# The output's transposes moved from TensorE to VectorE, in 32x32 blocks, with stores in 256-byte pieces

## The chip, the cores and the metric

The kernel runs on one core of a Trainium2 chip. The metric is device time in microseconds (us) of that core, as the median over several executions.

A core has five engines that matter here: TensorE (PE, with its weight loads shown as PEld), VectorE (DVE), ScalarE (ACT), GpSimd (POOL) and SyncE (SP), which issues most of the DMA transfers (1026 of 1214 in the trace of the kernel before).

## The reference

```python
X = np.fft.rfft(x, axis=1)                      # x: 8 batches x 3008 tokens x 256, fp32
y = np.fft.irfft(X * (filt_r + 1j * filt_i), n=3008, axis=1)
h = y.reshape(24064, 256) @ w_in                # w_in: 256 x 2048
g = np.where(h > 0, h, np.exp(np.minimum(h, 0)) - 1)
out = g @ w_out                                 # w_out: 2048 x 256, out: 24064 x 256
```

The kernel does the Fourier filter as matmuls with tables, and the two large products by a seven-product (Strassen-like) scheme.

## The kernel before

Its main loop has 192 steps, called quarters here: 8 batches, 6 groups of 512 tokens (448 in the first group), 4 quarters of the hidden layer. In each quarter PE interleaves seven groups of w_in matmuls (up: "U", into pha, phb, phc, phd, which are banks of PSUM, the memory that receives matmul results) with seven groups of w_out matmuls of the quarter before (down: "D", into po). DVE and ACT do the sums and the activation (ELU, the g of the reference) between them.

```python
for k in "UDUDUDUUD":            # first part of a quarter
    ...
for fn, a in plan.get((i, 0), ()):   # place 0: work planned here, as o_unit
    fn(*a)
for k in "UDUDD":                # second part: s3 (phc again), D, s4 (phd again), D, D
    ...
# in up_steps, in this order: s5: add("t4", mm(5, "c", True), g["t2"])     reads phc
#                             s7: add("b22", mm(7, "d", True), g["t4"])    reads phd
#                             s3: add("b12", mm(3, "c", False), g["t2"])   mm accumulates into phc
```

After the fourth quarter of a group, DVE forms c, the group's result with output columns on the partitions and tokens along the free dimension. One quarter later, at place 0, the output unit puts it the other way round and stores it. There are 48 units; the first is in quarter 5, and then there is one in every fourth quarter.

```python
def o_unit(b, m):
    c = cs_.pop((b, m))                               # two tiles [128, 512]
    for a in range(2):
        ps = psM.tile([P, 2, D], FP32, tag="mx", name="pso")
        o = op.tile([P, 2, D], FP32, tag="o%d" % a, name="o%d" % a)
        ...
                nc.tensor.transpose(ps[0:w, u, ts(dh, P)], c[dh][:, ds((2 * a + u) * P, w)], eye)
        nc.scalar.activation(out=o[:, 0:full, :], in_=ps[:, 0:full, :], func=AXT.Copy)
        ...
                nc.sync.dma_start(raw(out, ...), r[:, u:u + w, :])    # rows of 1 KB
```

## Time and profile before

The median of three runs is 2761.48 us (2761.05 to 2762.83).

| engine | busy us | share of the span |
|---|---|---|
| PE | 2667.8 | 97% |
| DVE | 2017.9 | 73% |
| ACT | 1332.3 | 48% |
| all DMA queues | | about 31% of 16 engines' time |

From the page, the chain that ended last by line, and the DMA queue of SyncE and its kin (packets, MB, share of 16 engines):

```profile
PE po L385 37%; PE pha L312 11%; PE phc L312 11%; PE phd L312 11%; PE phb L312 5%; PE psa L167 3%; PE psn L266 2%; PE psr L211 2%; PE pva L211 2%; PE pso L424 2%; DMA z<-t 1%; DVE g L317 1%; ACT e L323 1%; ACT e L324 1%; DVE c L403 1%
...
q1 hardware_dynamic: 122656, 173.60, 24.6%
```

The chain is matmuls almost throughout. The transposes (pso) have 2% of it, so that is about the most that their removal can bring. DMA is far from full.

### The profile page before, as it was taken

How to read it: one execution, taken by the hardware profiler on the slowest of the kernel's cores; microseconds unless marked ns; L12 is line 12 of the kernel's file. 1: busy time of each engine (PE TensorE's matmuls, PEld its weight loads, DVE VectorE, ACT ScalarE, POOL GpSimd, SP SyncE). 2: the span in 40 equal slices, each digit the busy share in tenths (PEclk: the TensorE clock that was granted, in tenths of full speed). 3: DMA queues.
4: the chain of work that ended last, by engine and by line, in shares of the span. 5: the costliest groups of instructions: out<-in, count | busy, mean ns of one | idle time of the engine just before them, and what ended most of it. 6: DMA issues, size and time to landing. Idle time of an engine off the chain costs nothing.

```text
span 2761.7 us, 36475 instructions
## 1 busy us (share of the span) xinstructions
PE 2667.8 (97%) x13376; PEld 2281.5 (83%) x13376; DVE 2017.9 (73%) x3427; ACT 1332.3 (48%) x2281; POOL 275.3 (10%) x325
## 2 busy tenths in 40 slices
PE   3689999999999999999999999999999999999998
PEld 1278778987899878998789877898789987899887
DVE  4877877777776777767776787767877677777776
ACT  2244455544455444554454544454454544554544
POOL 4311210002000120001200021000210012000000
PEclk7599999999999999999999999999999999999999
DMA  9644421434114331242313332143321223110100
GB/s 243 180 115 120 106 56 29 118 87 99 43 47 117 77 90 37 72 114 71 78 50 87 87 89 66 37 106 94 98 61 39 72 69 94 37 39 19 25 22 16
DMA packets 141634, 214.51 MB, mean 78 GB/s; under 512 B 25268, under 2 KB 99142, under 8 KB 141456
## 3 DMA queue, kind: packets, MB, share of 16 engines
q1 hardware_dynamic: 122656, 173.60, 24.6%
q0 software_dynamic: 17792, 36.93, 5.5%
q8 instruction: 106, 1.74, 0.3%
q10 hardware_dynamic: 1008, 1.64, 0.2%
q14 instruction: 72, 0.59, 0.1%
HBM read 137.04 MB, written 78.12 MB: 78 GB/s over the span
## 4 chain that ended last, share of the span: by engine, by line
PE 86%; DVE 7%; ACT 3%; DMA 2%; issue 2%; ACTq 0%; DVEq 0%; POOL 0%; SPq 0%
PE po L385 37%; PE pha L312 11%; PE phc L312 11%; PE phd L312 11%; PE phb L312 5%; PE psa L167 3%; PE psn L266 2%; PE psr L211 2%; PE pva L211 2%; PE pso L424 2%; DMA z<-t 1%; DVE g L317 1%; ACT e L323 1%; ACT e L324 1%; DVE c L403 1%
## 5 line engine op out<-in xcount | busy, mean ns | idle before, releaser
L385 PE MATMUL po<-g,wo 128*128 128x256 f32 (+1 forms) x5376 | 1324.2, 375 | 0.0
L385 PEld LDWEIGHTS po<-g,wo 128*128 128x128 f32 x5376 | 1021.4, 190 | 116.2
L323 ACT ACTIVATE e<-g 128x512 f32<-128x512 f32 (+1 forms) x576 | 357.6, 621 | 600.5 <-DVE g L317 600.3
L324 ACT ACTIVATE e<-e 128x512 f32<-128x512 f32 (+1 forms) x768 | 477.6, 622 | 24.4
L312 PE MATMUL pha<-y,wi 128*128 128x256 f32 (+1 forms) x1536 | 396.6, 381 | 9.3 <-ACT g L332 9.1
L317 DVE TENSOR_TENSOR g<-phc,g 128x512 f32<-128x512 f32 (+1 forms) x384 | 259.8, 677 | 197.5 <-PE phc L312 197.5
L328 DVE SCALAR_TENSOR_TENSOR g<-e,g 128x512 f32<-128x512 f32 (+1 forms) x576 | 387.5, 673 | 11.6 <-ACT e L324 11.2
L323 ACT ACTIVATE e<-pha 128x512 f32<-128x512 f32 (+1 forms) x192 | 113.0, 588 | 532.2 <-PE pha L312 532.2
L312 PEld LDWEIGHTS pha<-y,wi 128*128 128x128 f32 x1536 | 285.4, 191 | 93.4 <-ACT t L238 34.3
L317 DVE TENSOR_TENSOR g<-phd,g 128x512 f32<-128x512 f32 (+1 forms) x384 | 261.2, 680 | 86.4 <-PE phd L312 65.7
L328 DVE SCALAR_TENSOR_TENSOR g<-e,pha 128x512 f32<-128x512 f32 (+1 forms) x192 | 129.5, 674 | 259.7 <-ACT e L324 259.7
L227 POOL TENSOR_TENSOR sr<-sr,sp 128x512 f32<-128x512 f32 x64 | 80.9, 1264 | 1303.7 <-DVE sp L225 1303.7
L312 PE MATMUL phc<-ys,wi 128*128 128x256 f32 (+1 forms) x768 | 195.5, 377 | 2.8 <-DVE si L224 2.8
L312 PE MATMUL phd<-y,wi 128*128 128x256 f32 (+1 forms) x768 | 195.2, 377 | 1.3
L312 PE MATMUL phb<-ys,wi 128*128 128x256 f32 (+1 forms) x768 | 194.1, 375 | 0.0
L312 PE MATMUL phc<-y,wi 128*128 128x256 f32 (+1 forms) x768 | 194.0, 375 | 0.0
L312 PE MATMUL phd<-ys,wi 128*128 128x256 f32 (+1 forms) x768 | 193.7, 375 | 0.0
L312 PEld LDWEIGHTS phc<-ys,wi 128*128 128x128 f32 x768 | 145.3, 191 | 24.0 <-issue 8.1
L312 PEld LDWEIGHTS phd<-y,wi 128*128 128x128 f32 x768 | 145.2, 191 | 22.5 <-PE phc L312 6.5
L332 ACT ACTIVATE g<-pha 128x512 f32<-128x512 f32 (+1 forms) x192 | 112.7, 587 | 105.7 <-PE pha L312 105.5
L312 PEld LDWEIGHTS phb<-ys,wi 128*128 128x128 f32 x768 | 146.0, 190 | 17.1 <-issue 0.5
L312 PEld LDWEIGHTS phd<-ys,wi 128*128 128x128 f32 x768 | 145.8, 190 | 16.5
(108 smaller groups left out, 2787.9 us busy)
## 6 DMA issues: line engine op xcount, KB each, us to landing
z<-t SPq DMA_DIRECT2D x192, 128.0 KB, 3.9
t<-z SPq DMA_DIRECT2D x128, 192.0 KB, 3.7
yd<-t SPq DMA_DIRECT2D x128, 192.0 KB, 2.8
t<-yd SPq DMA_DIRECT2D x192, 128.0 KB, 4.2
out_dram<-o SPq DMA_DIRECT2D x176, 128.0 KB, 2.4
xc<-in_x_dram SPq DMA_DIRECT2D x84, 256.0 KB, 4.6
f<-fd POOLq DMA_DIRECT2D x112, 192.0 KB, 3.6
tn<-tn_t SPq DMA_DIRECT2D x48, 256.0 KB, 4.1
```

The source lines that it names most:

```text
L167: nc.tensor.matmul(ps[:, u, :], w[:, r + u, :], xt[:, r + u, :], start=True, stop=True)
L211: nc.tensor.matmul(ps[:, u:u + w, :], table[k, v, :], rhs[k, u:u + w, :], start=True, stop=True)
L227: nc.gpsimd.tensor_tensor(out=sr, in0=sr, in1=p, op=ALU.subtract)
L266: nc.tensor.matmul(ps[:, ts(q, P)], t[:, i - 4 * m, ds(dh * P, P)], w[:, i - 4 * m, :], start=True, stop=True)
L312: nc.tensor.matmul(banks[key][:, a, 0:h], w_in[q][:, COMBO[n], a, :], y[n], start=start and a == 0, stop=True, skip_group_check=True)
L317: nc.vector.tensor_tensor(out=g[o], in0=i0, in1=i1, op=ALU.add)
L323: nc.scalar.activation(out=e, in_=src, func=AXT.Relu, scale=-1.0)
L324: nc.scalar.activation(out=e, in_=e, func=AXT.Exp, scale=-1.0)
L328: nc.vector.scalar_tensor_tensor(out=g[n], in0=es[n], scalar=1.0, in1=src, op0=ALU.subtract, op1=ALU.max)
L332: nc.scalar.activation(out=g["t1"], in_=mm(1, "a", True), func=AXT.Copy)
L385: nc.tensor.matmul(po[i][:, u, 0:h], w_out[q][:, COMBO[n], a, :], g[n][:, a, :], start=q == 0 and a == 0 and n in (1, 3, 6, 4), stop=True, ...
L424: nc.tensor.transpose(ps[0:w, u, ts(dh, P)], c[dh][:, ds((2 * a + u) * P, w)], eye)
```

## The change

The intent is to take the transposes off PE, the engine that bounds the kernel, and the copies off ACT. The new layout takes a DVE transpose of 128x512 fp32 to turn each 32x32 block by itself, inside its group of 32 partitions. After that, partition group a (32 partitions) holds, for 32 tokens at a time, 32 columns from each half of c. The columns of w_out are therefore laid out so that these 64 columns are neighbours in the output, columns 64a to 64a+63. A token's 1 KB row then lies in four partition groups and leaves in four pieces of 256 bytes, in separate DMA issues: 16 or 24 stores of 32 KB a unit (24 KB and 8 KB in the first group), where there were 4 or 5 of mostly 128 KB.

```diff
-    eye = glob.tile([P, P], FP32, name="eye")
...
-            c = [kp.tile([P, 512], FP32, tag="c%d" % i, name="c%d" % i) for i in range(2)]
+            c = kp.tile([P, 2, 512], FP32, tag="c", name="c")
...
     def o_unit(b, m):
         c = cs_.pop((b, m))
-        for a in range(2):
-            ps = psM.tile([P, 2, D], FP32, tag="mx", name="pso")
...
-                    nc.tensor.transpose(ps[0:w, u, ts(dh, P)], c[dh][:, ds((2 * a + u) * P, w)], eye)
-            nc.scalar.activation(out=o[:, 0:full, :], in_=ps[:, 0:full, :], func=AXT.Copy)
...
+        o = op.tile([P, 16, 2, 32], FP32, tag="o", name="o")
+        for j, n in ((0, 8), (8, 6 if m == 0 else 8)):
+            nc.vector.transpose(out=o[:, j:j + n], in_=c[:, :, ds(32 * j, 32 * n)].rearrange("p e (j s) -> p j e s", s=32))
+        o = o.rearrange("p (u f k) e s -> p u f k (e s)", u=4, f=2)
...
+                for k in range(2):
+                    for a in range(4):
+                        nc.sync.dma_start(raw(out, b * N + n1 + 32 * N1 * k,
+                                              [[N1 * D, 32], [-D if f else D, w], [1, 64]], 64 * a),
+                                          o[ts(a, 32), u:u + w, f, k])
...
-            f, e = (t.rearrange("p (i c) -> p i c", i=4) for t in (f, e.bitcast(FP32)))
+            f, e = (t.rearrange("p (i a e s) -> p i e a s", i=2, a=4, e=2) for t in (f, e.bitcast(FP32)))
+            dst = dst.rearrange("p (i e) (a s) -> p i e a s", i=2, a=4)
```

More of the change, by code (lines that the diff above doesn't have):

```diff
@@ L110 @@
     ]
-    id_d = nc.inline_tensor(np.eye(P, dtype=np.float32), name="id_t").ap()
     def pool(name, bufs, **kw):
@@ L142, with raw @@
     xs, tas, tns, t1s, t2s, ss, t3s, t4s, zs, yds, ys, g_of, po_of, cs_ = ({} for _ in range(14))
-    def raw(src, row, ap):
-        return bass.AP(tensor=src.tensor, offset=src.offset + row * D, ap=ap)
+    def raw(src, row, ap, col=0):
+        return bass.AP(tensor=src.tensor, offset=src.offset + row * D + col, ap=ap)
     def x_load(b, c, queue=nc.sync, place=None):
@@ L398, in tail @@
             p35, p7 = (k[1][:, u, 0:h] for u in range(2))
-            c = [kp.tile([P, 512], FP32, tag="c%d" % i, name="c%d" % i) for i in range(2)]
-            (c11, c12), (c21, c22) = ((t[:, 0:h], t[:, h:2 * h]) for t in c)
+            c = kp.tile([P, 2, 512], FP32, tag="c", name="c")
+            (c11, c12), (c21, c22) = ((c[:, i, 0:h], c[:, i, h:2 * h]) for i in range(2))
             def add(o, i0, i1):
@@ L416, in o_unit @@
         c = cs_.pop((b, m))
-        for a in range(2):
-            ps = psM.tile([P, 2, D], FP32, tag="mx", name="pso")
-            o = op.tile([P, 2, D], FP32, tag="o%d" % a, name="o%d" % a)
-            full = 1 if m == 0 and a == 1 else 2
-            for u in range(2):
-                w = P if u < full else 64
-                for dh in range(2):
-                    nc.tensor.transpose(ps[0:w, u, ts(dh, P)], c[dh][:, ds((2 * a + u) * P, w)], eye)
-            nc.scalar.activation(out=o[:, 0:full, :], in_=ps[:, 0:full, :], func=AXT.Copy)
-            if full == 1:
-                nc.scalar.activation(out=o[0:64, 1, :], in_=ps[0:64, 1, :], func=AXT.Copy)
-            i0, i1 = order(m)[2 * a:2 * a + 2]
-            for f in range(2):
-                r = o[f * 64:f * 64 + 64]
-                for u, w in ((0, 2),) if i1 == i0 + 1 else ((0, 1), (1, 1)):
-                    i = (i0, i1)[u]
-                    if f and i == 0:
-                        continue
-                    n1 = N1 - i if f else i
-                    nc.sync.dma_start(raw(out, b * N + n1, [[N1 * D, 64], [-D if f else D, w], [1, D]]), r[:, u:u + w, :])
+        o = op.tile([P, 16, 2, 32], FP32, tag="o", name="o")
+        for j, n in ((0, 8), (8, 6 if m == 0 else 8)):
+            nc.vector.transpose(out=o[:, j:j + n], in_=c[:, :, ds(32 * j, 32 * n)].rearrange("p e (j s) -> p j e s", s=32))
+        o = o.rearrange("p (u f k) e s -> p u f k (e s)", u=4, f=2)
+        for u, w, i in ((0, 3, 1), (3, 1, 0)) if m == 0 else ((0, 4, 4 * m),):
+            for f in range(1 if i == 0 else 2):
+                n1 = N1 - i if f else i
+                for k in range(2):
[3 more added lines that the diff above has]
+                                          o[ts(a, 32), u:u + w, f, k])
     wds = {}
@@ L468, in w_convert @@
         m, e = (kp.tile([P, 512], U32, tag=t, name=n) for t, n in (("k0", "wm"), ("k1", "we")))
-        f, l = (kp.tile([P, 512], FP32, tag=t, name=n) for t, n in (("c0", "wf"), ("c1", "wl")))
+        fl = kp.tile([P, 2, 512], FP32, tag="c", name="wfl")
+        f, l = fl[:, 0], fl[:, 1]
         nc.vector.tensor_scalar(out=m, in0=hi, scalar1=0x000FFFFF, scalar2=None, op0=ALU.bitwise_and)
@@ L485, in w_convert @@
         else:
-            f, e = (t.rearrange("p (i c) -> p i c", i=4) for t in (f, e.bitcast(FP32)))
-        nc.vector.tensor_tensor(out=dst, in0=f, in1=e, op=ALU.mult)
+            f, e = (t.rearrange("p (i a e s) -> p i e a s", i=2, a=4, e=2) for t in (f, e.bitcast(FP32)))
+            dst = dst.rearrange("p (i e) (a s) -> p i e a s", i=2, a=4)
+        if shape:
+            nc.vector.tensor_tensor(out=dst, in0=f, in1=e, op=ALU.mult)
+        else:
+            for i in range(2):
+                nc.vector.tensor_tensor(out=dst[:, i], in0=f[:, i], in1=e[:, i], op=ALU.mult)
         if j % 2 == 1:
@@ L578 @@
             w_fetch(k)
-        nc.scalar.dma_start(eye, id_d)
         n_unit(0, 0)
```

## The prediction

> **What bounds the kernel now.** I read the page first: the busy shares, then the chain of waits that ended last.
>
> ```profile
> PE 2667.8 (97%) x13376; PEld 2281.5 (83%) x13376; DVE 2017.9 (73%) x3427; ACT 1332.3 (48%) x2281; POOL 275.3 (10%) x325
> ...
> PE 86%; DVE 7%; ACT 3%; DMA 2%; issue 2%; ACTq 0%; DVEq 0%; POOL 0%; SPq 0%
> ```
>
> TensorE holds 86% of the chain, and its 40 slices read 9 from the fourth on. What counts is time between matmul starts, not the busy sum. From about 215 us on, starts are 216 ns apart for a 256-column matmul, and the gaps above the usual pace sum to about 25 us over the remaining 2540 us, outside the filter matmuls. Time taken out of PE's stream there shortens the run one for one, unless something else is late at that point.
>
> Next, the groups by shape, for the two instructions that go, and the issues of the output tile:
>
> ```profile
> L424 PE MATMUL pso<-eye,c 128*128 128x128 f32 x368 | 48.5, 273 | 2.0 <-DVE g L317 1.2 <-DVE c L403 0.7
> ...
> L425 ACT ACTIVATE o<-pso 128x512 f32<-128x512 f32 x88 | 47.3, 584 | 3.7 <-PE pso L424 3.7
> ...
> L436 SPq DMA_DIRECT2D out_dram<-o x200: 467/604/2078, 218.7 to 2757.9; - x100
> ```
>
> The mean of 273 ns is a transpose's length; its cost is in the timeline of PE around one output unit, then of DVE there:
>
> ```profile
> 1258.60 1.03 PE L385 MATMUL po<-g,wo 128*128 128x256 f32 x4
> 1259.46 1.04 PE L424 MATMUL pso<-eye,c 128*128 128x128 f32 x8
> 1260.34 1.03 PE L312 MATMUL phc<-y,wi 128*128 128x256 f32 x4
> ...
> 1259.06 0.69 DVE L317 TENSOR_TENSOR g<-phc,g 128x512 f32<-128x512 f32 x1
> 1259.85 0.69 DVE L317 TENSOR_TENSOR g<-phd,g 128x512 f32<-128x512 f32 x1
> 1261.40 0.69 DVE L317 TENSOR_TENSOR g<-phc,g 128x512 f32<-128x512 f32 x1 [0.86 <-PE phc L312]
> ```
>
> Eight transposes hold PE from 1259.46 to 1260.34, 0.87 us, 109 ns each. I measured this at all 48 units: 0.87 us at 46, 1.19 at the first, and the last lies in the tail. On DVE, an add reads bank phc and ends at 1259.75, and after the next add DVE is idle 0.86 us until PE has filled phc again. The new transposes go into that idle slot. But the PE group that follows, the second one into phc, accumulates into the bank the first add reads, so it cannot start before 1259.75. Today the transposes cover that.
>
> Last, the tail:
>
> ```profile
> 2754.46 0.42 DVE L403 TENSOR_TENSOR c<-k,k 128x256 f32<-128x256 f32 x1
> ...
> 2755.19 1.08 ACT L425 ACTIVATE o<-pso 128x512 f32<-128x512 f32 x2 [3.65 <-PE pso L424]
> 2755.81 2.71 SPq L436 DMA_DIRECT2D out_dram<-o  x4
> ```
>
> The last block of c is complete at 2754.88, the last of four stores is issued at 2757.9, and the span ends at 2761.7.
>
> [...] No transpose on DVE is in this trace; the 128x512 fp32 add[...] takes 677 ns, so I take 0.68 us for a 128x512 transpose, an estimate. [...] The trace has no 256 B stores; its 1 KB packets take 46 ns at the median.
>
> **The change part by part.**
> *Removed from PE:* 384 transposes. In the stream 47 units x 0.87 = 40.9 us; the 48th is in the tail.
> *Removed from ACT:* 104 copies, some 53 us, on no path except once in the tail. Two PSUM buffers per unit are also no longer taken from the shared pool of four. I went through the rotation: a later group gets its bank from an earlier one in every case, or one freed some 4 us before it is wanted. Neither gain nor loss.
> *Added to DVE:* 96 transposes of 0.68 us, 65 us in all, DVE from 73% to about 76%. Per unit, two of them start 0.6 us apart[...].
> *What PE gives back:* without the transposes the second phc group waits for the add into t4 that reads phc. Relative to the start of the transposes, that add ends in an ordinary batch at -0.67, +0.29, -0.16, -0.16, +0.10 and -0.41 us over the six units. A wait also costs some 0.15 us: 0.05 from the release to the start (seen in the tail) and 0.1 because the weight load is no longer hidden (PE groups of four after a wait last 1.13 us instead of 1.03). So two units of six lose: 0.44 + 0.25 = 0.69 us a batch, 4.8 us over seven batches. In the last batch, where TensorE has less other work, five units lose (0.51, 0.29, 0.28, 0.28, 0.26, each + 0.15): 2.4 us; the unit before them 0.6; and at the first unit (1.14 late) all 0.87 is lost. Sum 8.7 us. PE's net gain is 40.9 - 8.7 = 32.2 us.
> *What DVE's delay does:* the next add from phc starts after the transposes, at about +2.4 us instead of +1.94, and PE is up to 0.87 us earlier, so it is late by about 0.9 us against PE. The add after it, from phd, is late by about 0.4. What PE needs next from these are the combined operands: b22 about 3 us, t1 about 2.8 us before its matmul in the ordinary quarter. DVE waits for ACT or PE between 1 and 3 us in each quarter, so it catches up. I count nothing.
> *Stores:* 104 a batch of 32 KB instead of 25 of mostly 128 KB: 832 issues for 200. The issue's median is 0.6 us with 128 pieces, and the new ones also have 128 pieces. A burst of 16 keeps the SyncE queue for about 10 us of a quarter of 12 to 14. The loads and the spectrum stores behind it come later by up to 8 us, but they are issued two quarters (about 26 us) before use. Nothing in the steady part.
> *Tail:* two transposes after 2754.88 (1.3 us), then 15 issues of 0.6 us before the last: issued 10.4 us after c is complete, instead of 3.0. The stretch from there to the end stays 3.8 us. Tail: +7.4 us.
> *Weights:* eight products for w_out become two of half size, 0.7 instead of 0.6 us; about five are on the chain at the start: +0.5 us.
> Sum: 2761.5 - 32.2 + 7.4 + 0.5 = 2737. I leave 1 us for what I did not see: 2738.
>
> **Rivals.**
> First, *DVE becomes the limit*. For it: in the quarters with filter products DVE has 13 operations of 0.6 to 0.7 us, four products and, one in four, seven adds and a transposed unit, about 12 us on average of PE's 14. If the fp32 transpose took twice my estimate, a unit would add 2.8 us on DVE. Against it: PE's operands come nearly 3 us early. It would make 2745 to 2765.
> Second, *the stores stop the SyncE queue*. For it: at the start the spectrum stores take 1.1 us per issue instead of 0.58[...]; 16 x 1.1 is 17.6 us, longer than a quarter, and loads would then slip from unit to unit. Against it: the queue waits in more than half of the span (859 us of it for the ACT copies of the output), and DMA is 30% busy. Four times the packets would add some 3 to 6% of DMA time, if a 256 B packet costs between half and all of a 1 KB one. It would make 2745 to 2790.
> Third, *PE gets all 41 us back*, because DVE in its turn moves forward with PE: 2728 with the tail, 2720 if the tail costs nothing.
>
> **Range and chances.** A gain of over 2% needs less than 2706 us, and all of the transposes with no tail give 2720: 2%. Over 2% slower means 2817, which takes a queue that stops PE some 1.7 us per unit beyond all that it saves: 3%. Within 2%: 95%. The range, 2722 to 2760, has the third rival at its lower end and mild forms of the other two at its upper.
>
> **What would show it right or wrong.** The group pso is gone from PE. After the po group, the second phc group starts with no gap at four units of six and with a gap of 0.3 to 0.4 us at two, released by DVE's add. The DVE transposes last about 0.68 us, and DVE's idle time before the next phc add disappears. SyncE's stores show 16 issues of about 0.6 us, and the last is issued about 10 us after c is complete. I am wrong if a transpose lasts well over 1 us, if an issue of a store takes over 1 us in the steady part, if PE's gaps behind z, t or yd loads grow, or if gaps at combined operands (g on DVE) appear in the quarter after a unit.

## The result, and the profile after

The changed kernel takes 2734.93 us (2733.8 to 2735.32, 4 runs) against 2761.5 us, 26.6 us less. The ratio is 0.9902, 95% interval 0.9885 to 0.9919: a clear gain of 1%, within the 2% that counts as the same. A ratio is the mean time of one kernel's runs over that of the other's of the same rounds, so it is not quite the ratio of the medians.

In the page after, the busy shares, the chain by engine, and the DMA queue (the changed kernel's line numbers are about two lower in the main loop: L310 for L312, L315 for L317, L383 for L385):

```profile
PE 2626.5 (96%) x12992; PEld 2237.5 (82%) x12992; DVE 2066.9 (76%) x3531; ACT 1286.0 (47%) x2177; POOL 275.6 (10%) x325
...
q1 hardware_dynamic: 210592, 173.65, 25.8%
...
PE 77%; DVE 12%; ACT 5%; DMA 2%; issue 2%; POOL 0%; DVEq 0%; SPq 0%; ACTq 0%; POOLq 0%
```

PE has lost exactly the 384 transposes (13376 less 12992) and 41 us of busy time; DVE has gained 49 us. The chain goes through DVE more often, 12% of the span instead of 7%: there are now places where PE waits for DVE, and a chain that follows such a wait back stays on DVE for a while. SyncE's queue moved 88 thousand packets more for 1.2 points of DMA time.

The new instructions, first the DVE transposes in the groups by shape (count, busy us, mean ns, idle before):

```profile
L421 DVE STREAM_TRANSPOSE o<-c 128x512 f32<-128x512 f32 x88 | 57.4, 687 | 0.2
```

Then the stores, in the view of tile o (count, then ns of one issue: least, median, most):

```profile
L429 SPq DMA_DIRECT2D out_dram<-o x832: 315/430/2152, 216.7 to 2730.9; - x167
```

The timeline of PE, then of DVE, around the unit that the prediction shows (start, us):

```profile
1244.55 1.03 PE L310 MATMUL phd<-y,wi 128*128 128x256 f32 x4
1245.41 1.03 PE L383 MATMUL po<-g,wo 128*128 128x256 f32 x4
1246.61 1.13 PE L310 MATMUL phc<-y,wi 128*128 128x256 f32 x4 [0.17 <-DVE g L315]
...
1245.87 0.68 DVE L315 TENSOR_TENSOR g<-phc,g 128x512 f32<-128x512 f32 x1
1246.66 0.69 DVE L315 TENSOR_TENSOR g<-phd,g 128x512 f32<-128x512 f32 x1
1247.27 1.29 DVE L421 STREAM_TRANSPOSE o<-c 128x512 f32<-128x512 f32 x2
1248.49 0.65 DVE L315 TENSOR_TENSOR g<-phc,g 128x512 f32<-128x512 f32 x1
```

The second phc group follows the po group without transposes between. It starts at 1246.61, 1.20 us after the po group's start, where the usual distance is 0.86: PE stood still for 0.34 us, until DVE's add from phc had ended at 1246.55. The bracket's 0.17 is less, because a matmul's length reaches past the next one's start: a group of four is 1.03 us long, and the next starts after 0.86. The group also lasts 1.13 us instead of 1.03; its first weight load starts with it, at 1246.61, where the one of the po group starts 0.21 us ahead of its group (1245.20). On DVE the idle 0.86 us are gone, filled by the transposes.

The tail, on DVE and on SyncE:

```profile
2722.24 0.41 DVE L401 TENSOR_TENSOR c<-k,k 128x256 f32<-128x256 f32 x1
2722.57 1.30 DVE L421 STREAM_TRANSPOSE o<-c 128x512 f32<-128x512 f32 x2
...
2723.89 7.43 SPq L429 DMA_DIRECT2D out_dram<-o  x16
```

The 16 issues take 7.43 us, 0.46 each.

To place the gain I cut both spans at three points that both kernels have: the start of the second phc group in quarters 4 and 6 (the first unit lies between them), and the end of the last block of c. The same table holds the experiments, one profiled execution each. The last column is the median of all runs; an execution's time is some 1.8 us over the profile's span.

| kernel | start to quarter 4 | quarter 4 to 6 | quarter 6 to last c | tail | median |
|---|---|---|---|---|---|
| before | 201.79 | 30.00 | 2523.09 | 6.83 | 2761.48 |
| after | 200.56 | 31.70 | 2490.40 | 10.78 | 2734.93 |
| e1, after again | 199.96 | 31.68 | 2490.54 | 10.78 | 2734.65 |
| e2, PE reordered | 199.38 | 29.14 | 2482.45 | 10.77 | 2723.86 |
| e3, last stores on two queues | 201.48 | 31.68 | 2490.55 | 7.28 | 2732.78 |
| e4, e2 and e3 | 200.15 | 29.13 | 2482.45 | 7.30 | 2721.58 |
| e5, transposes back on PE | 200.96 | 29.99 | 2522.71 | 11.21 | 2766.67 |
| e6, DVE transposes twice | 200.15 | 31.69 | 2497.85 | 12.26 | 2744.33 |
| e7, four times | 201.04 | 31.69 | 2616.11 | 15.24 | 2865.63 |
| e8, before with small stores | 199.45 | 30.00 | 2523.05 | 14.04 | 2769.07 |
| e9, after, fills on POOL | 200.44 | 27.37 | 2490.88 | 10.78 | 2730.90 |
| e10, e4, fills on POOL | 202.50 | 27.37 | 2482.58 | 7.27 | 2720.00 |

From before to after: 1.23 us less, 1.70 more, 32.69 less, 3.95 more; the sum is 28.3 us less. The first column scatters by 3 us over all the kernels, and by 2.3 us between before and e8, which have the same instructions there. Nothing in it is laid to the change. The other columns repeat to 0.5 us where nothing was changed, so small effects are read from them and not from the medians.

### The profile page after: what moved, and what is told of

It reads as the page before. It is cut to its first block, busy times and chain, and to the rows that moved or that the text cites. A ratio compares the mean times of both kernels' runs of the same rounds, so it can differ in the third digit from the quotient of the medians.

```text
span 2733.4 us, 36388 instructions
## 1 busy us (share of the span) xinstructions
PE 2626.5 (96%) x12992; PEld 2237.5 (82%) x12992; DVE 2066.9 (76%) x3531; ACT 1286.0 (47%) x2177; POOL 275.6 (10%) x325
## 4 chain that ended last, share of the span: by engine, by line
PE 77%; DVE 12%; ACT 5%; DMA 2%; issue 2%; POOL 0%; DVEq 0%; SPq 0%; ACTq 0%; POOLq 0%
PE po L383 34%; PE pha L310 11%; PE phc L310 10%; PE phd L310 10%; PE phb L310 5%; DVE g L315 3%; PE psa L165 3%; ACT e L322 2%; ACT e L321 2%; PE pva L209 2%; PE psn L264 2%; PE psr L209 2%; DVE c L401 2%; DVE g L326 1%; DVE g L359 1%
## 5 line engine op out<-in xcount | busy, mean ns | idle before, releaser
L383 PE MATMUL po<-g,wo 128*128 128x256 f32 (+1 forms) x5376 | 1325.1, 375 | 0.0
L383 PEld LDWEIGHTS po<-g,wo 128*128 128x128 f32 x5376 | 1022.0, 190 | 116.4
L310 PE MATMUL pha<-y,wi 128*128 128x256 f32 (+1 forms) x1536 | 396.2, 380 | 9.3 <-ACT g L330 9.2
L315 DVE TENSOR_TENSOR g<-phc,g 128x512 f32<-128x512 f32 (+1 forms) x384 | 257.7, 671 | 141.3 <-PE phc L310 141.3
L310 PEld LDWEIGHTS pha<-y,wi 128*128 128x128 f32 x1536 | 285.3, 190 | 93.3 <-ACT t L236 34.1
L315 DVE TENSOR_TENSOR g<-phd,g 128x512 f32<-128x512 f32 (+1 forms) x384 | 260.6, 679 | 70.1 <-PE phd L310 50.0
L310 PE MATMUL phc<-y,wi 128*128 128x256 f32 (+1 forms) x768 | 196.3, 378 | 5.0 <-DVE g L315 5.0
L310 PE MATMUL phc<-ys,wi 128*128 128x256 f32 (+1 forms) x768 | 195.3, 377 | 2.6 <-DVE si L222 2.6
L310 PE MATMUL phd<-y,wi 128*128 128x256 f32 (+1 forms) x768 | 194.7, 376 | 1.3
L310 PE MATMUL phd<-ys,wi 128*128 128x256 f32 (+1 forms) x768 | 194.2, 375 | 0.0
L310 PE MATMUL phb<-ys,wi 128*128 128x256 f32 (+1 forms) x768 | 193.8, 375 | 0.4 <-DVE ys L288 0.4
L310 PEld LDWEIGHTS phc<-y,wi 128*128 128x128 f32 x768 | 140.6, 190 | 29.5 <-DVE g L315 13.3
L310 PEld LDWEIGHTS phc<-ys,wi 128*128 128x128 f32 x768 | 145.3, 191 | 23.7 <-issue 7.8
L310 PEld LDWEIGHTS phd<-y,wi 128*128 128x128 f32 x768 | 144.7, 190 | 22.4 <-PE phc L310 6.5
L310 PEld LDWEIGHTS phd<-ys,wi 128*128 128x128 f32 x768 | 146.4, 191 | 16.7
```

Source lines behind the costliest of these rows:

```text
L310: nc.tensor.matmul(banks[key][:, a, 0:h], w_in[q][:, COMBO[n], a, :], y[n], start=start and a == 0, stop=True, skip_group_check=True)
L315: nc.vector.tensor_tensor(out=g[o], in0=i0, in1=i1, op=ALU.add)
L383: nc.tensor.matmul(po[i][:, u, 0:h], w_out[q][:, COMBO[n], a, :], g[n][:, a, :], start=q == 0 and a == 0 and n in (1, 3, 6, 4), stop=True, ...
```

## The experiments

The theory: the kernel runs at PE's pace. The transposes gave their time back, except where PE now waits for one DVE add; DVE's extra work is absorbed; the small stores cost only in the tail. The rivals: the gain comes from the ACT copies; DVE or the stores cost something everywhere; the waits have another cause. e1 to e4 ran on one chip together, e5 to e8 on another, then e9 and e10. All outputs are correct.

**e1: the changed kernel again.** No edit.

> The changed kernel as it is, for comparison on the same chip: 2735 us, 26 to 27 us under the kernel before.

Measured: 2734.65 us, ratio 0.9899 (0.9884 to 0.9914). It repeats.

**e2: a w_out group where the transposes stood.**

```diff
-            for k in "UDUDD":
+            for k in ("DUDUD" if i % 4 == 1 and i >= 5 else "UDUDD"):
```

> In every quarter with an output unit, one group of w_out matmuls moves ahead of the second group into phc, to the place where the transposes stood. If PE's 20 waits in the stream are waits for DVE's add that reads phc (my theory: 5.8 us of gaps and some 2.6 us of matmuls with exposed weight loads), they go and nothing else changes: 2727 us, between 2725 and 2729. If the gaps come from something else (a PSUM bank, DVE being late as a whole), the time stays at 2735 or the gaps move to another place.

Measured: 2723.86 us, ratio 0.9859 (0.9844 to 0.9873), 10.8 us under e1. In the stretch from quarter 6 to the last c it is 8.09 us shorter than e1. PE at the same unit as above, then DVE:

```profile
1239.58 1.89 PE L383 MATMUL po<-g,wo 128*128 128x256 f32 x8
1241.31 1.03 PE L310 MATMUL phc<-y,wi 128*128 128x256 f32 x4
...
1240.05 0.68 DVE L315 TENSOR_TENSOR g<-phc,g 128x512 f32<-128x512 f32 x1
```

Two w_out groups stand together now. When they are done the add is over (1240.73), and the phc group starts on time and at its usual length, 1.03 us. All 20 waits of the steady part are gone, and no other appeared. So the waits were for this add. The 8.09 us fit the 5.8 us of gaps and 2.0 us of longer groups that I count in the changed kernel's trace there. The whole gain is larger than the expected 8 us; most of the rest lies between quarters 4 and 6 (2.54 us), and e9 tells why.

**e3: the last unit's stores on two queues.**

```diff
+                        queue = nc.scalar if b == B - 1 and m == 5 and a % 2 else nc.sync
-                        nc.sync.dma_start(raw(out, ...), ...)
+                        queue.dma_start(raw(out, ...), ...)
```

> The stores of the very last output unit are issued from SyncE and ScalarE in turn, 8 each, instead of 16 from SyncE. If the tail is set by issuing at 0.46 us each, it shortens by 8 x 0.46 = 3.7 us: 2731 us. If it is set by the landing of 256-byte pieces, it stays at 2735.

Measured: 2732.78 us, ratio 0.9892 (0.9876 to 0.9909); only 1.9 us under e1, half of what was expected. The tail itself did shorten by 3.5 us, from 10.78 to 7.28. SyncE's part of it:

```profile
2724.96 3.68 SPq L430 DMA_DIRECT2D out_dram<-o  x8
```

So that part of the tail is issue time. In the profiled run the stretch before quarter 4 was 1.5 us longer than in e1, which is within that stretch's scatter. That accounts for that run; for the medians it is likely and not shown.

**e4: both.** The edits of e2 and e3.

> Both edits of the two runs before. If the two losses are separate, they add: 8.4 + 3.7 us under the changed kernel, 2723 us (2721 to 2726), about 38 us under the kernel before.

Measured: 2721.58 us, ratio 0.985 (0.9835 to 0.9865). The columns show both effects side by side, unchanged: 2482.45 in the steady part and 7.30 in the tail.

**e5: the transposes back on PE, for nothing.** `eye` is loaded again; nobody reads pso.

```diff
+        for h in range(2):
+            ps = psM.tile([P, 2, D], FP32, tag="mx", name="pso")
+            for u in range(2):
+                w = 64 if m == 0 and h == u == 1 else P
+                for dh in range(2):
+                    nc.tensor.transpose(ps[0:w, u, ts(dh, P)], c[:, dh, ds((2 * h + u) * P, w)], eye)
         o = op.tile([P, 16, 2, 32], FP32, tag="o", name="o")
```

> The changed kernel with the 384 transposes put back on PE; nothing reads their result, there are no ACT copies, and the output still comes from DVE. If the gain is PE time alone, it is given back: 40 us of transposes less the 8.4 us of waits they cover: 2766 us (2763 to 2769). If the gain came from the missing ACT copies, it stays near 2735.

Measured: 2766.67 us, ratio 1.002 (1.0007 to 1.0032). The steady stretch is 2522.71 us, 32.2 more than in e1 and within 0.4 of the kernel before, although the ACT copies are still missing, DVE still transposes and the stores are still small. In the steady stretch the gain is PE time alone.

**e6: each DVE transpose twice.**

```diff
+            for _ in range(2):
                 nc.vector.transpose(out=o[:, j:j + n], ...)
```

> Every DVE transpose is done twice: 1.3 us more on DVE for each of 48 units. My theory has it absorbed by DVE's idle time: 1.3 us in the tail and at most 3 us elsewhere, 2736 to 2740 us. If DVE's work is on the path: 48 x 1.3 = 62 us more, 2797 us.

Measured: 2744.33 us, ratio 0.9939 (0.9927 to 0.9952), 9.7 us over e1: more than I had allowed, and far from 62. The tail has 1.5 us of it, the steady part 7.3. Of that, 4.8 us are one wait of PE a batch. Where it occurs, the timeline of DVE, ACT and PE:

```profile
330.49 2.79 DVE L422 STREAM_TRANSPOSE o<-c 128x512 f32<-128x512 f32 x4
...
335.74 0.63 ACT L322 ACTIVATE e<-e 128x512 f32<-128x512 f32 x1
336.28 0.58 ACT L236 ACTIVATE t<-pva 128x512 f32<-128x512 f32 x1
...
336.91 1.13 PE L310 MATMUL pha<-y,wi 128*128 128x256 f32 x4 [0.62 <-ACT t L236]
```

DVE's lateness passes to ACT: its exponentials come late, and the copy that frees PE's next bank stands behind them in the same queue. PE waits for that copy, and pha starts 0.69 us later than at its usual distance, in seven batches. The way runs through a third engine, and I had not followed it. Some 2.6 us more are 0.37 us a batch in the quarter after the second unit, where PE's phd group comes late while DVE is still at its filter products; what releases it was not followed. In the changed kernel, with single transposes, the wait for ACT does not occur.

**e7: four times.** The same edit with `range(4)`.

> Every DVE transpose is done four times: 3.9 us more on DVE per unit. The slack of about 3 us should be used up in part of the units: 3.9 us in the tail and up to 1 us per unit, 2739 to 2790 us. If DVE is the bound: 48 x 3.9 = 187 us more, 2922 us.

Measured: 2865.63 us, ratio 1.0374 (1.036 to 1.0388), 131 us over e1 and past the 55 that I had allowed at most, though not the 187 of a bound DVE. A stretch of it, as us, then busy us and count of PE, PEld, DVE, ACT and POOL, then the granted clock, the DMA share and GB/s:

```profile
340.00:360.00 20.00, 19.11 (x80) 13.25 (x80) 15.24 (x25) 9.27 (x16) 3.49 (x4) 0.83 0.58 126
```

The mean granted clock in this stretch is 0.83, and 0.969 in the whole run, for 0.977 in e1. Behind the waits PE's clock is at half for 3.4 or 6.8 us at a time, eleven times from quarter 6 to the last c, 44 us in all. That can account for at most 22 of the 126 us that this stretch is longer than in e1; the rest was not broken down.

**e8: the kernel before, with small stores alone.**

```diff
-                    nc.sync.dma_start(raw(out, ..., [1, D]]), r[:, u:u + w, :])
+                    for e in range(4):
+                        nc.sync.dma_start(raw(out, ..., [1, 64]], 64 * e), r[:, u:u + w, ts(e, 64)])
```

> The kernel before, with its stores alone cut to 256-byte pieces in 16 issues a unit; transposes stay on PE, copies on ACT. My theory: nothing in the steady part, and in the tail 16 issues of 0.46 us for 4 of 0.68, less 0.8 us of landing: +3.9 us, 2765 us. If the small stores hold up the queue or DMA: 2772 us or more.

Measured: 2769.07 us, ratio 1.0029 (1.0015 to 1.0042), 7.6 us more. All of it is in the tail, 14.04 for 6.83; the steady part is 2523.05 for 2523.09. So the small stores cost nothing there. My 3.9 us for the tail failed on the time of an issue:

```profile
2753.43 10.39 SPq L437 DMA_DIRECT2D out_dram<-o  x16
```

That is 0.65 us each, where the changed kernel's issues take 0.46 with as many pieces of the same size. Here a store spans 64 partitions with two pieces each, there 32 with four. Why that matters was not tried.

**e9: the filter buffers' fills on GpSimd.** They come just ahead of the first unit.

```diff
-            at(4, 1, nc.vector.memset, f, 0.0)
+            at(4, 1, nc.gpsimd.memset, f, 0.0)
```

> The changed kernel with three fills of the filter buffers (1.07 us apart, just ahead of the first output unit) on GpSimd instead of DVE. In the changed kernel PE waits 2.5 us there and the granted clock then falls to half for 3.4 us. If the wait is DVE's lateness and the clock follows from the wait, both go: the stretch between the second phc groups of quarters 4 and 6 falls from 31.7 to about 28.2 us, the rest is unchanged: 2731 us. If the half clock has nothing to do with the wait, it stays and only the 2.5 us go: about 29.5 us in that stretch.

Measured: 2730.9 us, ratio 0.989 (0.9875 to 0.9906). Between quarters 4 and 6 it takes 27.37 us for 31.68 in e1 (28.2 was expected). What happens there in the changed kernel, in PE's timeline:

```profile
211.47 1.03 PE L383 MATMUL po<-g,wo 128*128 128x256 f32 x4
214.86 1.45 PE L310 MATMUL phc<-y,wi 128*128 128x256 f32 x4 [2.37 <-DVE g L315]
216.10 1.91 PE L383 MATMUL po<-g,wo 128*128 128x256 f32 x4
```

A stretch of 3 us there in the changed kernel, with the columns as in e7, and then the same groups in e9's timeline of PE:

```profile
216.00:219.00 3.00, 3.00 (x8) 2.37 (x8) 1.85 (x4) 2.16 (x4) 1.61 (x4) 0.51 0.62 123
```

```profile
211.35 1.03 PE L383 MATMUL po<-g,wo 128*128 128x256 f32 x4
212.21 1.03 PE L310 MATMUL phc<-y,wi 128*128 128x256 f32 x4
213.07 1.03 PE L383 MATMUL po<-g,wo 128*128 128x256 f32 x4
```

PE is idle for 2.37 us, and then the granted clock is half for 3.4 us (0.51 in this stretch): a po group lasts 1.91 us, where in e9 it lasts 1.03. Half of 3.4 us is 1.7 us, which is what the table shows for this stretch from before to after. In e2 the wait at this place is 1.50 us and the clock does not fall; in e9 there is no wait and no fall. So here the half clock came with the wait and went with it, and together they cost 4.3 us. In e1, e3, e6 and e7 the wait of 2.4 us and the half clock of 3.4 us stand here as well. The length of one wait does not settle it: in e7 no wait from quarter 6 to the last c is over 1.46 us, and yet the clock falls there eleven times, though not after most waits of that length. What decides it was not tried.

**e10: e4 with the fills on GpSimd.**

> The same on top of the reordered kernel with two queues for the last stores. There the wait was 1.7 us without a fall of the clock (29.1 us in that stretch): about 1 us less than that kernel, 2720 to 2721 us.

Measured: 2720.0 us, ratio 0.9851 (0.9837 to 0.9864) against the kernel before at 2761.57. It beats both kernels: 41.6 us under the one, about 15 under the other. The gain over e4 is 1.6 us in the medians and 1.8 in the stretch.

## Why the prediction was right

*It came out within its range.* 2738 was said, 2734.93 measured; 2722 to 2760 was the range. The main term was right for its reasons, and smaller terms were off, in both directions. The tail cost 3.45 us less than was said; the first unit cost 1.70 us more. The first is the larger, and most of the 3 us between 2738 and 2734.93 is the balance of the two and the 1 us that was left for the unseen. That they partly cancel is luck.

*Removed from PE.* The 40.0 us of the 46 steady units are gone, and e5, which puts them back, returns the time with them. That ACT's copies lie on no path in the steady part held as well. What a transpose cost PE was the distance between starts and not its length: 273 ns long, they start 109 ns apart.

*What PE gives back.* Right in place, cause and size. The six units of an ordinary batch were to lose at two: PE's gaps are 0.34 and 0.15 us at just those, and each waiting group lasts 0.1 us longer, so 0.44 and 0.25 as worked out. Over the steady part there are 20 waits of 5.8 us and 2.0 us of longer groups, 7.8 in sum, as predicted without the first unit. e2 removes them and finds 8.1. The sign "a gap of 0.3 to 0.4 us at two" is met by the first of the two only.

*DVE's delay.* "I count nothing" held: 40.0 less 7.8 is 32.2, and the stretch got 32.69 shorter. The transpose's 0.68 us was an estimate, taken from an add with no DVE transpose in the trace; 0.687 was measured, beside 0.682 and 0.690 for the fp32 adds of 128x512 that read phc and phd. At the unit shown the next phc add starts 2.22 us after the time at which PE's transposes would have begun (1246.27); the +2.4 said for it rested in part on an estimate that no trace showed. But the reason given, that operands come 3 us early, was too generous. e6 shows that 1.5 us more a unit already cost 7.3 us in the steady part, 4.8 of them by way of ACT's queue.

*Stores.* Nothing in the steady part: right (e8). One sign of being wrong did show, an issue of over 1 us: 22 of the 832 took that long, up to 2.15 us. e8 has 24 such issues, and its steady part is no longer for them. DMA time rose by 1.2 points and not by the 3 to 6 that the second rival gave it; a 256-byte packet takes 21 ns at the median, less than half of the 46 ns of 1 KB. Per byte that is 1.8 times as long, so such pieces are slower for their size here.

*Tail.* The term was +7.4 us and measured +3.95. The mis-sized step is "15 issues of 0.6 us": they take 0.47. And "the stretch from there to the end stays 3.8 us" failed: it is 2.5 us. Why is not shown: in e8, whose last store is as small, it is 3.3 us. That the issues make the tail was right (e3).

*First unit.* "All 0.87 is lost" was too mild: 1.70 us were lost beyond that. The wait was foreseen; that PE's clock falls to half after it was not, and half of those 3.4 us is the 1.70.

*Weights.* The +0.5 us could not be seen under a start that scatters by 3 us. It stays open.

*Rivals.* The first, DVE as the limit, did not come about, but its figure for a transpose of twice the length, 2745 to 2765, lies near e6's 2744. The second falls with e8; the 1.1 us per issue that it named are the mean distance of issues at the start (24 in 27.1 us), waits for earlier transfers included, and one issue is 0.30 to 0.64 us long there. The third, all 41 us back, is what e2 makes of the change, and that kernel goes lower than the 2728 given for it, mostly because the tail costs less than was said.

## What to carry to other kernels

Work that is taken off a bound engine may have been covering a wait. Look at what stands behind it in that engine's order, read when its operand is ready, and put other ready work in the gap: one swapped group brought 11 us of the 42 that the best version gains. Take the slack of a helper engine from the longest way round, through the queues of the other engines, and not from the direct operands alone: 4.8 of e6's 7.3 us in the steady part came by that way. And count DMA issues where nothing runs beside them: at the end of the program 16 small stores cost 4 us that the same stores cost nowhere else.
